# Linear attention and a highway layer on one core: each pair of output tiles stored by one transfer

## The chip, the cores and the metric

The kernel runs on one core of a Trainium2 chip. The metric is the device time of one execution in microseconds; lower is better. The kernel before takes 126.87 us, the median of three runs (126.06 to 127.11). A trace of one execution was taken by the hardware profiler; all durations below come from it.

The names of the engines in the profile are PE (TensorE, matrix products), PEld (its weight loads), DVE (VectorE), ACT (ScalarE), POOL (GpSimd) and SP (SyncE, which here only issues transfers). Transfers between DRAM and the on-chip memory SBUF run on the core's 16 DMA engines, whoever issues them. In this kernel SP and ACT issue them.

## The reference

Inputs are q, k and v of shape (8, 8, 576, 64), that is batch, heads, tokens, head width, in float32, and two weights of 512 x 512 with a bias of 512. First comes linear attention, for each batch and head:

```python
q_s = softmax(q, axis=-1)            # over the head width
k_s = softmax(k, axis=2)             # over the tokens
kv  = einsum('bhsd,bhse->bhde', k_s, v)
x   = einsum('bhsd,bhde->bhse', q_s, kv)
```

Then the heads are put side by side, which gives x of shape (4608, 512), and a highway layer follows:

```python
H = maximum(x @ w_h, 0)
T = sigmoid(x @ w_t + b_t)
out = T * H + (1 - T) * x            # (4608, 512), float32
```

## The kernel before

**Tokens and tiles.** A batch has 576 tokens, cut as 64 groups p of 9 tokens j: token 9p + j. A load of q, k or v puts two heads times the 64 groups on the 128 partitions, with four pairs of heads and nine tokens along each partition (`rows_of`, L182). The output is computed in 36 tiles of 128 tokens by 512 columns. For one batch there are four tiles jp = 0 to 3, each of 64 groups times two tokens (rows 0 to 63 hold one token of each group, rows 64 to 127 another). The ninth tokens of two batches make one tile together. So two batches are nine tiles, and four such rounds are 36.

**Steps.** Each batch passes these steps: `k`, `v`, `q` load it; `ek` and `eq` take exponentials on ACT; `vc` casts v to half precision on POOL, ACT or DVE; `kv` (L254) multiplies on TensorE; `kr` and `kn` divide by the sums; `qt` (L292) turns the exponentials of q with TensorE transposes, and `qc` (L301) copies them to SBUF on DVE or ACT. Each tile i then passes `xu` (L318, q times kv), `rs` and `x` (L333, division by the sums, giving x in half precision), `xt` (L340) and `xe` (L347), which turn x, `mt` (L367, times w_t) and `mh` (L375, times w_h), `th` (tanh of half the gate), `dd`, and then `uu` and `oo` (L426), which combine the parts into the output. Where a step `uu` has the suffix P, the product (L408) and one sum (`ee`, L401) run on POOL, otherwise a single DVE instruction (L410) takes their place. `fill` steps (L172) multiply zeros on TensorE, while data is still on the way.

**Stores.** Two neighbouring tiles share one output buffer of two times 512 columns (`mate`, L414; `oo` writes half of it). Tiles 31 to 34 are stored singly, and the last tile (35, ninth tokens) in two halves of its columns. Step `st` (L428) stores. For a pair it is called twice, with r = 0 and r = 1, and each call stores 64 partitions, with two tokens of each group that lie two apart. A single tile is also stored in two calls of 64 partitions. A tile of ninth tokens goes in one call of 128 partitions. The output buffers of pairs are seven (pool `op`, shared with the four landing buffers of the weights at the start); those of single tiles are three (L420).

**Order.** The list `ORDER` (L16) is the program: its steps are emitted one after the other, and every engine and every queue works through its own part of it in that order. A suffix A, D or P picks the engine. Nothing is reordered later. A store with suffix A is issued by ACT, all others and all loads by SP; an instruction that waits for its data holds back all that stand behind it on the same queue. Loads have three landing buffers for each of q, k and v.

Of the kernel before, what the change touches and what calls it, by code (L numbers as in the profile page):

```python
# [16 lines left out]
b_0 b_32 setuppool fill_30 fill_30 k_0_2 setupdve bsplit v_0_2 bp v_0_0 vc_0_0:D vc_0_1:D ek_0_2 k_0_0 vc_0_3:A ek_0_3
vc_0_2 kv_0_1 bc ek_0_0 kr_0_1 q_0_0 q_0_4 w_t_0 ek_0_1 kn_0_1 fill_30 w_h_2 kv_0_0 eq_0_0 bw_0 qt_0_0 kr_0_0 qc_0_0
kn_0_0 bw_1 eq_0_1 fill_16 w_h_0 xu_0_1 xu_0_0 xu_1_0 qt_0_1 w_t_2 fill_16 wtc_0 rs_0_1 rs_1_0 rs_0_0 q_1_0 x_1_0 whc_2
qc_0_1:A x_0_0 half v_1_0 xt_0_0 xe_0_0 x_0_1 xt_0_1 whd_3 whd_2 xe_0_1:D mt_0_0 xt_1_0 whc_0 k_1_0 wtc_2:D vc_1_1 k_1_2  # L20
xe_1_0 v_1_2 eq_0_2 whd_0 xu_3_0 eq_1_0 mh_0_1 vc_1_0 mt_0_1 q_1_4 mt_1_0 rs_3_0 q_2_0 x_3_0 th_0_0 ek_1_1 xu_2_0 whd_1
xt_3_0 ek_1_0 mh_0_0 rs_2_0 xe_3_0:D qt_1_0 bw_3 x_2_0 mh_1_0 dd_0 k_2_0 ee_0 xt_2_0 mh_3_0 vc_1_2 kv_1_0 v_2_0 dd_1
xe_2_0:D qc_1_0 th_1_0 ek_1_2 ek_1_3 mh_2_0 uu_0_0:P kr_1_0 mt_3_0 uu_1_0 vc_1_3:A bw_2 dd_3 qt_0_2 kn_1_0 th_3_0 oo_0_0
kv_1_1 mt_2_0 oo_1_0 bw_5 xu_4_0 uu_3_0:P kr_1_1 q_3_0 kn_1_1 qc_0_2 dd_2 xu_5_0 rs_5_0 eq_1_1 th_2_0 x_5_0 rs_4_0
qt_1_1 xt_5_0 x_4_0 xe_5_0:D qc_1_1:A bw_4 xu_6_0 ee_3 eq_1_2 xu_4_1 qt_1_2 rs_6_0 qc_1_2 eq_2_1 eq_2_2 xt_4_0 uu_2_0:P
xe_4_0 rs_4_1 k_3_0 x_6_0 x_4_1 mh_5_0 mt_5_0 xu_7_0 xt_4_1 dd_5 xe_4_1:D eq_2_0 mt_4_0 th_5_0 ek_2_2 qt_2_0 xt_6_0
rs_7_0 x_7_0 mt_4_1 ek_2_0 xu_8_0 xe_6_0:D uu_5_0 qc_2_0 xt_7_0 oo_3_0 mh_4_0 th_4_0 mh_6_0 rs_8_0 ee_2 oo_5_0 bw_6:A
xe_7_0:D vc_2_0:A x_8_0 mh_4_1 v_3_0 k_4_0 vc_2_2 mt_6_0 th_6_0 xt_8_0 kv_2_0 dd_6 dd_4 bw_7:A uu_6_0 kr_2_0 xe_8_0
kn_2_0 oo_2_0 mh_7_0 uu_4_0:P mt_7_0 dd_7 xu_9_0 ee_4 bw_8:A qt_2_1 rs_9_0 oo_4_0 eq_3_1 th_7_0 v_4_0 mt_8_0 x_9_0
xt_9_0 bw_9:A qc_2_1 eq_3_0 xu_10_0 ek_3_2 mh_8_0 q_4_0 xe_9_0:D rs_10_0 x_10_0 mt_9_0 dd_8 xu_11_0 qt_2_2 rs_11_0  # L30
xt_10_0 th_8_0 uu_7_0:P oo_6_0 x_11_0 ek_3_0 mh_9_0 vc_3_0 qc_2_2 uu_8_0 xe_10_0 xu_12_0 qt_3_0 xt_11_0 rs_12_0 vc_3_2:A
x_12_0 bw_10:A ee_7 dd_9 mh_10_0 xe_11_0:D v_5_0 th_9_0 kv_3_0 mt_10_0 bw_11:A qc_3_0 ek_4_2 st_1_0_0 ee_9 kr_3_0
xt_12_0 th_10_0 oo_7_0 oo_8_0 kn_3_0 qt_3_1 xe_12_0:D xu_13_0 k_5_0 eq_3_2 uu_9_0:P rs_13_0 x_13_0 st_3_0_1 oo_9_0
bw_12:A mh_11_0 mt_11_0 ek_4_0 th_11_0 dd_10 q_5_0 xu_14_0 vc_4_2 xt_13_0 xe_13_0 dd_11 rs_14_0 mt_12_0 uu_10_0:P
th_12_0 x_14_0 qc_3_1 mh_12_0 xu_15_0 vc_4_0:A eq_4_0 uu_11_0 rs_15_0 qt_3_2 x_15_0 mh_13_0 dd_12 xt_14_0 bw_13:A
xe_14_0:D kv_4_0 xt_15_0 eq_4_1 uu_12_0 qc_3_2 ee_10 st_1_0_1:A mh_14_0 kr_4_0 xe_15_0:D bw_14:A mt_13_0 kn_4_0 xu_16_0
th_13_0 oo_10_0 oo_11_0 eq_4_2 dd_13 v_6_0 rs_16_0 qt_4_0 x_16_0 qc_4_0:A uu_13_0 mt_14_0 oo_12_0 xt_16_0 xe_16_0
bw_16:A xu_17_0 dd_14 qt_4_1 mh_16_0 rs_17_0 k_6_0 x_17_0 vc_5_2 xu_18_0 qc_4_1 mh_15_0 th_14_0 rs_18_0 x_18_0 oo_13_0
bw_15:A mt_15_0 ee_14 ek_5_2 xu_20_0 ek_5_0 vc_5_0 xt_18_0 xe_18_0 dd_16 rs_20_0 x_20_0 mt_16_0 th_15_0 dd_15 xt_17_0
kv_5_0 th_16_0 xe_17_0:D mh_18_0 uu_14_0:P uu_16_0:P kr_5_0 q_6_0 eq_5_2 bw_18:A oo_14_0 uu_15_0 xt_20_0 kn_5_0 ee_16  # L40
qt_5_2 eq_5_1 mt_18_0 bw_17:A xe_20_0 qc_5_2 xu_19_0 dd_18 qt_4_2 th_18_0 rs_19_0 oo_15_0 x_19_0 qc_4_2:A uu_18_0
mh_17_0 mt_17_0 xt_19_0 eq_5_0 bw_20:A st_3_0_0 xu_21_0 q_7_0 dd_17 qt_5_0 th_17_0 xe_19_0:D qc_5_0:A rs_21_0 oo_16_0
mh_20_0 vc_6_0 uu_17_0 x_21_0 mt_20_0 bw_19:A ek_6_2 st_7_0_0 vc_6_2 dd_20 xt_21_0 xu_22_0 th_20_0 rs_22_0 bw_21:A
mt_19_0 st_5_0_0 xe_21_0 mh_19_0 oo_17_0 st_5_0_1 x_22_0 ek_6_0 xu_23_0 qt_5_1 rs_23_0 xt_22_0 eq_6_0 mh_21_0 x_23_0
xe_22_0:D kv_6_0 ee_20 dd_19 st_7_0_1 xt_23_0 v_7_0 uu_20_0:P dd_21 oo_18_0 qc_5_1 th_19_0 mt_21_0 th_21_0 ee_19 qt_6_0
bw_22:A k_7_0 st_14_0_1:A st_10_0_1 st_10_0_0 kr_6_0 kn_6_0 mh_22_0 uu_19_0:P uu_21_0 xu_24_0 xe_23_0:D rs_24_0 mt_22_0
st_8_0_0 eq_7_0 oo_19_0 th_22_0 x_24_0 qc_6_0 mh_23_0 bw_23:A oo_20_0 dd_22 xu_25_0 rs_25_0 qt_7_0 x_25_0 uu_22_0:P
eq_6_1 qc_7_0:A xt_24_0 mt_23_0 xe_24_0:D xu_26_0 dd_23 xt_25_0 th_23_0 st_12_0_0 oo_21_0 rs_26_0 x_26_0 qt_6_1 ee_22
xe_25_0 uu_23_0 mh_24_0 xt_26_0 vc_7_0 qc_6_1 xu_27_0 bw_24:A oo_22_0 rs_27_0 x_27_0 eq_7_1 mt_24_0 qt_7_1 xe_26_0
bw_25:A xu_29_0 th_24_0 bw_26:A rs_29_0 dd_24 ek_7_0 mt_25_0 st_21_0_0 x_29_0 mh_25_0 vc_7_2 dd_25 xt_27_0 ek_7_2  # L50
xu_28_0 mh_26_0 th_25_0 oo_23_0 rs_28_0 eq_7_2 st_14_0_0 mt_26_0 qc_7_1 st_21_0_1:A qt_7_2 x_28_0 xe_27_0 ee_24 th_26_0
uu_24_0:P kv_7_0 uu_25_0 bw_27:A mh_27_0 xt_28_0 dd_26 kr_7_0 kn_7_0 xe_28_0 eq_6_2 mt_27_0 oo_24_0 ee_26 xu_30_0
mh_28_0 st_12_0_1 uu_26_0:P dd_27 bw_28:A xt_29_0 mt_28_0 th_27_0 oo_25_0 qc_7_2:A rs_30_0 x_30_0 uu_27_0 st_23_0_1
xu_31_0 dd_28 xe_29_0 bw_29:A mh_29_0 xt_30_0 st_23_0_0:A rs_31_0 th_28_0 mt_29_0 x_31_0 xe_30_0 st_25_0_1 uu_28_0
xt_31_0 dd_29 xu_32_0 mh_30_0 th_29_0 st_19_0_1 bw_30:A rs_32_0 oo_26_0 x_32_0 st_16_0_1:A xe_31_0:D mt_30_0 st_19_0_0:A
xt_32_0 qt_6_2 th_30_0 oo_27_0 xu_33_0 st_17_0_0 dd_30 mh_31_0 oo_28_0 rs_33_0 bw_31:A xe_32_0 x_33_0 uu_29_0:P
st_26_0_0:A uu_30_0 mt_31_0 dd_31 xu_34_0 xt_33_0 ee_29 rs_34_0 qc_6_2:A bw_32:A st_28_0_1 xe_33_0:D mh_32_0 th_31_0
oo_29_0 st_16_0_0:A x_34_0 oo_30_0 mt_32_0 xu_35_0 uu_31_0 oo_31_0 xt_34_0 st_31_0_1 dd_32 th_32_0 uu_32_0 xe_34_0:D
st_28_0_0 mh_33_0 bw_33:A rs_35_0 mt_33_0 mh_34_0 bw_34:A x_35_0 dd_33 th_33_0 xt_35_0 uu_33_0 mt_34_0 st_31_0_0:A
xe_35_0:D oo_32_0 bw_35_1 dd_34 st_32_0_1 st_32_0_0 th_34_0 oo_33_0 mh_35_0 bw_35_0:A st_30_0_1 mt_35_1 st_25_0_0  # L60
uu_34_0 st_33_0_1:A th_35_1 st_30_0_0 dd_35 mt_35_0 th_35_0 st_33_0_0 uu_35_1 oo_34_0 oo_35_1 st_34_0_1 st_34_0_0:A
# [5 lines left out]
def kernel(  # L67
# [360 lines left out]
    def st(e, i, h, r):  # L428
        bs, jp = tiles[i]
        b = bs[r % len(bs)]  # L430
        cs, rows = columns(i, h), slice(NP * r, NP * r + NP)
        eng = nc.scalar if e == "A" else nc.sync
        dst = out[b * S:(b + 1) * S, cs].rearrange("(p j) n -> p j n", j=NJ)
        if mate(i) is not None:
            eng.dma_start(dst[:, 2 * jp + r - 2:2 * jp + r + 1:2], T[f"oo{i - 1}"][rows])
        elif len(bs) == 1:
            eng.dma_start(dst[:, 2 * jp + r], T[f"o{i}"][rows, cs])
        else:
            ends = out[b * S:(b + 2) * S, cs].rearrange("(r j) n -> r j n", j=NJ)
            eng.dma_start(ends[:, 8], T[f"o{i}"][:, cs])  # L440

# [40 lines left out]
```

## Time and profile before

| what | value |
|---|---|
| median of three runs | 126.87 us |
| the profiled execution's own time | 126.15 us |
| its span, first to last instruction | 124.40 us |
| TensorE busy | 113.7 us, 91% of the span |
| DVE, ACT, POOL busy | 97.4, 91.9, 87.7 us |
| read from DRAM, written | 30.41 MB, 9.44 MB |
| DMA packets | 20292 |

The page divides the span into 40 equal slices of 3.1 us; a digit is the busy share of an engine in tenths. Of the output's transfers, 28 carry pairs (256 KB each), eight carry single tiles (128 KB each), three carry ninth tokens (256 KB), and two the halves of the last tile (128 KB each). SP issues 29 of the 41 and ACT 12.

### The profile page before, as it was taken

Reading aid. Unit: us, or ns where it says so; the run is one execution under the profiler, and the core shown is the slowest. Engines: PE = TensorE matmul, PEld = TensorE weight load, DVE = VectorE, ACT = ScalarE, POOL = GpSimd, SP = SyncE. Lnnn points to the kernel's source line nnn. Section 1 sums busy time; section 2 is a strip of 40 time slices with the busy share of each in tenths; the row PEclk is TensorE's granted clock in tenths of the full one; section 3 lists DMA queues with packets and bytes.
Section 4 is the critical chain, followed back from the end, with each engine's and each line's share of the span. In section 5 each row is a group of like instructions: output and inputs, shape, how many; then the busy total and the mean of one; then the engine's idle time right before and its main releaser. Section 6 shows DMA issues by size and latency. Waiting matters only on the chain.

```text
span 124.4 us, 3617 instructions
## 1 busy us (share of the span) xinstructions
PE 113.7 (91%) x1447; PEld 71.3 (57%) x1447; DVE 97.4 (78%) x230; ACT 91.9 (74%) x144; POOL 87.7 (71%) x88
## 2 busy tenths in 40 slices
...
DMA  3999999999999999999999999999878309987993
GB/s 68 390 391 363 383 374 388 384 378 391 391 384 391 392 389 391 391 388 397 401 401 394 381 395 403 383 403 387 320 182 220 71 16 227 266 256 156 264 226 115
DMA packets 20292, 40.08 MB, mean 322 GB/s; under 512 B 1202, under 2 KB 3506, under 8 KB 20276
## 3 DMA queue, kind: packets, MB, share of 16 engines
...
q14 instruction: 5, 0.04, 0.1%
HBM read 30.41 MB, written 9.44 MB: 320 GB/s over the span
## 4 chain that ended last, share of the span: by engine, by line
PE 87%; DVE 5%; ACT 1%; issue 1%; POOL 0%; DVEq 0%; POOLq 0%
PE gps L375 24%; PE tps L367 24%; PE turned L172 12%; PE xu L318 7%; PE turned L340 7%; PE qps L292 6%; PE kv L254 5%; DVE u L410 1%; DVE d L395 1%; PE tps L357 1%; DVE x L333 1%; DVE o L426 1%; DVE w16t L206 0%; DVE w16h L212 0%; ACT tps L391 0%
## 5 line engine op out<-in xcount | busy, mean ns | idle before, releaser
L367 PE MATMUL tps<-w16t,xT 128*128 128x512 f16 (+1 forms) x148 | 37.1, 373 | 0.2 <-DVE w16t L206 0.2
L375 PE MATMUL gps<-w16h,xT 128*128 128x512 f16 x144 | 37.0, 379 | 0.0
L426 POOL TENSOR_TENSOR o<-u,x 128x512 f32<-128x512 f16 (+1 forms) x21 | 23.7, 1134 | 4.9 <-DVE u L410 4.9
L244 POOL CAST v<-v 128x1152 f16<-128x1152 f32 (+1 forms) x13 | 13.0, 1006 | 19.3 <-DMA v<-in_v_dram 19.3
L333 DVE TENSOR_TENSOR x<-xu,rs 128x512 f16<-128x512 f32 (+1 forms) x38 | 25.0, 660 | 1.9
L395 DVE SCALAR_TENSOR_TENSOR d<-x,gps 128x512 f16<-128x512 f16 x36 | 24.2, 678 | 0.8 <-PE gps L375 0.7
L367 PEld LDWEIGHTS <-xT 128*128 128x128 f16 x148 | 13.6, 98 | 12.5 <-issue 0.4
L238 ACT ACTIVATE ek<-k 128x1152 f16<-128x1152 f32 (+1 forms) x20 | 18.7, 963 | 2.4 <-DMA k<-in_k_dram 2.2
L401 POOL TENSOR_TENSOR e<-d,x 128x512 f16<-128x512 f16 x15 | 17.3, 1154 | 4.2 <-DVE d L395 4.2
L282 ACT ACTIVATE qe<-q 128x1024 f16<-128x1024 f32 (+1 forms) x24 | 19.9, 841 | 0.0
L375 PEld LDWEIGHTS <-xT 128*128 128x128 f16 x144 | 12.6, 98 | 10.3 <-DVE xT L347 0.3
L355 ACT COPY tps<-ball 128x512 f32<-128x512 f32 (+1 forms) x30 | 17.6, 585 | 0.5 <-DVE u L410 0.3
L408 POOL TENSOR_TENSOR u<-th,d 128x512 f16<-128x512 f16 x15 | 17.4, 1157 | 0.5 <-POOL u L408 0.4
L426 POOL TENSOR_TENSOR o<-u,e 128x512 f32<-128x512 f16 x15 | 17.3, 1153 | 0.6
L391 ACT ACTIVATE tps<-tps 128x512 f32<-128x512 f32 (+1 forms) x22 | 12.4, 562 | 7.1 <-PE tps L367 6.8
L172 PE MATMUL turned<-blank 128*128 128x256 f16 x122 | 15.9, 295 | 1.3 <-POOL blank L151 1.3
L410 DVE SCALAR_TENSOR_TENSOR u<-tps,d 128x512 f16<-128x512 f32 (+1 forms) x22 | 14.4, 660 | 1.4 <-ACT tps L391 0.6
L340 PE MATMUL turned<-idh,x 128*128 128x128 f16 x144 | 14.3, 219 | 1.3 <-DVE x L333 0.8
L172 PEld LDWEIGHTS <-blank 128*128 128x128 f16 x122 | 12.7, 106 | 3.7 <-POOL blank L151 1.3
L318 PE MATMUL xu<-kvb,eq 128*128 128x130 f16 (+1 forms) x160 | 14.2, 224 | 0.1
L340 PEld LDWEIGHTS <-x 128*128 128x128 f16 x144 | 10.1, 98 | 6.9 <-DVE x L333 2.2
L318 PEld LDWEIGHTS <-eq 128*128 128x128 f16 (+1 forms) x160 | 10.0, 101 | 6.7 <-DVE x L333 1.8
...
## 6 DMA issues: line engine op xcount, KB each, us to landing
...
out_dram<-o SPq DMA_DIRECT2D x23, 256.0 KB, 10.1
...
out_dram<-o ACTq DMA_DIRECT2D x8, 256.0 KB, 5.5
...
```

Of the source, the lines that this page charges most:

```text
L172: nc.tensor.matmul(spare, blank[:, 0:P], blank[:, 0:2 * P], start=True, stop=True, skip_group_check=True)
L238: nc.scalar.activation(t[:, :, c:c + n].rearrange("p j c d -> p c j d"), T[f"k32{b}"][:, c:c + n].rearrange("p c (j d) -> p c j d", j=NJ), ...
L282: nc.scalar.activation(t[:, j0:j1].rearrange("p j c d -> p c j d"), T[f"q32{b}"].rearrange("p c (j d) -> p c j d", j=NJ)[:, :, j0:j1], AF.Exp)
L318: nc.tensor.matmul(dst, T[f"eq{b}_{jp // 2}"][:, jp % 2, n], kvb[b % NKV][:, hh, kk], start=True, stop=True, skip_group_check=True)
L333: nc.vector.tensor_mul(t[:, k0:k1], sums(i, k)[:, :, :, 0:64], T[f"rs{i}_{k}"][:, 0:k1 - k0].unsqueeze(3).to_broadcast([P, k1 - k0, 4, D]))
L340: nc.tensor.matmul(t[:, n], T[f"x{i}"][:, n * P:(n + 1) * P], idh, is_transpose=True, start=True, stop=True, skip_group_check=True)
L355: nc.scalar.copy(t[:, cs], ball[:, cs])
L367: nc.tensor.matmul(T[gate(i, k)][:, cs], T[f"xT{i}"][:, n], w16["t"][:, n, cs], start=False, stop=(n == parts[-1] and not first), skip_gro ...
L375: nc.tensor.matmul(t, T[f"xT{i}"][:, n], w16["h"][:, n], start=(first and n == parts[0]), stop=(n == parts[-1] and not (first and len(part ...
L395: nc.vector.scalar_tensor_tensor(t, T[f"x{i}"], -0.5, T[f"gps{i}"], op0=ALU.mult, op1=ALU.max)
L408: eng.tensor_mul(t, T[f"th{i}"], T[f"d{i}"])
L426: eng.tensor_add(t[:, cs], T[f"u{i}"][:, cs], T[f"{'e' if lifted(i) else 'x'}{i}"][:, cs])
```

## The change

The two tokens of each group that share a tile are no longer neighbours: tile jp now holds tokens j and j + 2, so that the two tiles of a pair together give, in each partition of their common buffer, two tokens that lie side by side in DRAM, 4096 bytes. Step `st` loses its argument r. A pair is stored by one transfer of 128 partitions with 4096 bytes each (512 KB), a single tile by one transfer of 128 partitions with 2048 bytes each (256 KB). The tiles of ninth tokens are stored as before. That leaves 23 store steps, 19 on SP and 4 on ACT.

The list of steps is a new one. Its loads begin with q, v and k of batch 0 (before: k, v, k, q). It has 99 multiplications of zeros in its `fill` steps (before 122), 17 tiles with their product on POOL (before 15), and 12 copies of `qc` on ACT (before 8). The stores among the loads stand as follows, with the other steps left out:

```
... q_5_0 st_1_0 v_6_0 k_6_0 q_6_0 st_3_0:A q_7_0 st_5_0 k_7_0 st_7_0 st_10_0 v_7_0
st_19_0 st_21_0:A st_12_0 st_16_0 st_14_0 st_23_0 st_26_0 st_17_0 st_8_0:A st_25_0
st_28_0 st_31_0 st_33_0 st_30_0 st_32_0 st_34_0 st_35_0 st_35_1:A
```

A second way of turning q, by DMA transposes (`dt`), is defined as well, for batches named by steps `dt_` in the list. The list has no such step, so `BY_DMA` is empty.

```diff
     def qt(e, b, g):
...
                 nc.tensor.matmul(
-                    t[:, (j - j0) // 2, 2 * kk:2 * kk + 2, (j - j0) % 2],
+                    t[:, (j - j0) % 2, 2 * kk:2 * kk + 2, (j - j0) // 2],
                     T[f"qe{b}"][:, j, 2 * kk:2 * kk + 2].rearrange("p c d -> p (c d)"), idh,
...
+    def turned_q(b, jp, n):
+        if b not in BY_DMA:
+            return T[f"eq{b}_{jp // 2}"][:, jp % 2, n]
...
     def xu(e, i, k):
...
-                nc.tensor.matmul(dst, T[f"eq{b}_{jp // 2}"][:, jp % 2, n], kvb[b % NKV][:, hh, kk],
+                nc.tensor.matmul(dst, turned_q(b, jp, n), kvb[b % NKV][:, hh, kk],
...
-    def st(e, i, h, r):
+    def st(e, i, h):
         bs, jp = tiles[i]
-        b = bs[r % len(bs)]
-        cs, rows = columns(i, h), slice(NP * r, NP * r + NP)
+        b, cs = bs[0], columns(i, h)
         eng = nc.scalar if e == "A" else nc.sync
-        dst = out[b * S:(b + 1) * S, cs].rearrange("(p j) n -> p j n", j=NJ)
-        if mate(i) is not None:
-            eng.dma_start(dst[:, 2 * jp + r - 2:2 * jp + r + 1:2], T[f"oo{i - 1}"][rows])
-        elif len(bs) == 1:
-            eng.dma_start(dst[:, 2 * jp + r], T[f"o{i}"][rows, cs])
-        else:
+        if len(bs) == 2:
             ends = out[b * S:(b + 2) * S, cs].rearrange("(r j) n -> r j n", j=NJ)
             eng.dma_start(ends[:, 8], T[f"o{i}"][:, cs])
+            return
+        if mate(i) is None:
+            rows = out[b * S:(b + 1) * S].rearrange("(p j) n -> j p n", j=NJ)
+            a, step = (2 * jp, 1) if b in BY_DMA else (4 * (jp // 2) + jp % 2, 2)
+            eng.dma_start(rows[a:a + step + 1:step], T[f"o{i}"])
+        else:
+            rows = out[b * S:(b + 1) * S].rearrange("(p j) n -> p (j n)", j=NJ)
+            a = 4 * (jp // 2) * DM
+            eng.dma_start(rows[:, a:a + 4 * DM].rearrange("p (r n) -> r p n", r=2),
+                          T[f"oo{i - 1}"].rearrange("p a n -> p (a n)"))
```

More of the change, by code (lines that the diff above doesn't have):

```diff
@@ L16 @@
 ORDER = """
[L17 to L61, printed above, removed]
@@ L62 @@
-uu_35_0 oo_35_0:D st_35_0_0 st_35_1_0:A
+b_0 b_32 q_0_0 setuppool v_0_0 k_0_0 setupdve half eq_0_0 bsplit fill_16 k_0_2 fill_12 qt_0_0 bp ek_0_1 ek_0_0 fill_12
+fill_16 vc_0_1:A qc_0_0 fill_6 vc_0_0 ek_0_3 v_0_2 kv_0_0 vc_0_2:A kr_0_0 vc_0_3:D kn_0_0 fill_12 ek_0_2 q_0_4 kv_0_1
+eq_0_1 kr_0_1 kn_0_1 xu_0_0 w_t_0 fill_9 bc qt_0_1 xu_0_1 rs_0_1 xu_1_0 bw_0 w_h_2 rs_1_0 rs_0_0 w_t_2 q_1_0 eq_0_2
+fill_16 wtc_2:P wtc_0:D qc_0_1:A x_1_0 xt_1_0 x_0_0 whc_2 xu_3_0 bw_1 x_0_1 xe_1_0 w_h_0 xt_0_0 xt_0_1 v_1_0 xe_0_1
@@ new lines @@
+rs_3_0 xe_0_0 mt_1_0 mt_0_0 mt_0_1 k_1_0 x_3_0 xt_3_0 eq_1_0 whc_0 qt_1_0 th_0_0 vc_1_0 whd_0 bw_3 whd_1 k_1_2 whd_2
+whd_3 xu_2_0 xe_3_0 mh_0_0 mh_0_1 qc_1_0:A vc_1_1:D ek_1_1 v_1_2 mh_1_0 dd_0 rs_2_0 qt_0_2 ek_1_0 q_1_4 ee_0 x_2_0
+th_1_0 qc_0_2:A mt_3_0 ek_1_2 ek_1_3 dd_1 uu_0_0:P vc_1_3:A q_2_0 k_2_0 xt_2_0 vc_1_2 th_3_0 xe_2_0:D uu_1_0 mh_3_0 dd_3
+uu_3_0:P kv_1_0 bw_2 eq_1_1 mh_2_0 eq_1_2 kr_1_0 kv_1_1 kn_1_0 kr_1_1 v_2_0 mt_2_0 xu_4_0 bw_4 kn_1_1 xu_5_0 dd_2 qt_1_1
+rs_5_0 th_2_0 qc_1_1:A oo_0_0 ee_2 oo_1_0 rs_4_0 x_5_0 xu_4_1 ee_3 bw_5 uu_2_0:P x_4_0 rs_4_1 xt_5_0 q_3_0 xe_5_0:D
@@ new lines @@
+k_3_0 xu_6_0 mh_5_0 rs_6_0 x_4_1 xt_4_0 oo_3_0 xt_4_1 eq_2_0 mt_5_0 x_6_0 xe_4_0:D dd_5 mt_4_0 xu_7_0 xe_4_1:D mt_4_1
+rs_7_0 eq_2_1 th_5_0 xt_6_0 x_7_0 mh_4_1 mh_4_0 qt_1_2 eq_2_2 xe_6_0:D uu_5_0 qc_1_2 xt_7_0 ek_2_2 ek_2_0 oo_2_0 mh_6_0
+xu_8_0 dd_4 oo_5_0 rs_8_0 th_4_0 xe_7_0:D qt_2_0 bw_6:A x_8_0 mt_6_0 vc_2_0:A vc_2_2 bw_7:A v_3_0 th_6_0 uu_4_0:P bw_8:A
+qc_2_0 xt_8_0 kv_2_0 k_4_0 dd_6 mh_7_0 kr_2_0 kn_2_0 v_4_0 xe_8_0:D mt_7_0 dd_7 ee_6 eq_3_2 eq_3_1 uu_6_0:P xu_9_0 ee_4
+q_4_0 qt_2_1 v_5_0 rs_9_0 x_9_0 oo_4_0 mt_8_0 th_7_0 ee_7 xu_10_0 qc_2_1 oo_6_0 rs_10_0 xt_9_0 eq_3_0 x_10_0 mh_8_0
@@ new lines @@
+bw_9:A dd_8 xe_9_0 qt_2_2 xu_12_0 rs_12_0 x_12_0 mt_9_0 mh_9_0 xt_10_0 qc_2_2 vc_3_0 xe_10_0:D xu_11_0 uu_7_0:P ek_3_2
+rs_11_0 qt_3_0 th_8_0 ek_3_0 x_11_0 oo_7_0 uu_8_0 k_5_0 vc_3_2:A q_5_0 mh_10_0 dd_9 kv_3_0 kr_3_0 oo_8_0 xt_11_0 kn_3_0
+qc_3_0:A bw_10:A ee_9 st_1_0 xe_11_0:D qt_3_1 mt_10_0 th_9_0 qc_3_1:A dd_10 xu_13_0 bw_11:A xt_12_0 mh_11_0 v_6_0
+th_10_0 ek_4_0 mt_11_0 rs_13_0 x_13_0 xu_14_0 k_6_0 xe_12_0:D xt_13_0 uu_10_0 uu_9_0:P rs_14_0 mh_12_0 xe_13_0:D x_14_0
+bw_12:A dd_12 mt_12_0 th_11_0 dd_11 xu_15_0 bw_13:A vc_4_2 xt_14_0 th_12_0 oo_9_0 ek_4_2 eq_4_0 mt_13_0 mh_13_0 rs_15_0
@@ new lines @@
+x_15_0 xe_14_0:D xu_16_0 uu_12_0 oo_10_0 qt_3_2 q_6_0 rs_16_0 mh_14_0 bw_14:A xt_15_0 mt_14_0 dd_13 th_13_0 eq_4_2
+vc_4_0 x_16_0 dd_14 uu_13_0 uu_11_0:P st_3_0:A qc_3_2:A xe_15_0:D oo_12_0 eq_4_1 kv_4_0 qt_4_0 mh_15_0 kr_4_0 xt_16_0
+kn_4_0 oo_13_0 th_14_0 qc_4_0:A ee_11 xu_17_0 bw_15:A uu_14_0 xe_16_0:D rs_17_0 ek_5_2 qt_4_1 mt_15_0 vc_5_0 oo_11_0
+x_17_0 dd_15 ee_15 xu_18_0 bw_16:A vc_5_2 mh_16_0 th_15_0 qc_4_1 ek_5_0 rs_18_0 x_18_0 xt_17_0 xe_17_0:D mt_16_0
+uu_15_0:P xu_20_0 oo_15_0 q_7_0 eq_5_2 xt_18_0 rs_20_0 x_20_0 eq_5_0 qt_5_2 bw_17:A mh_17_0 xe_18_0 kv_5_0 th_16_0
@@ new lines @@
+xt_20_0 dd_16 dd_17 qc_5_2:A xe_20_0 mt_17_0 qt_4_2 kr_5_0 uu_16_0 kn_5_0 mh_20_0 qc_4_2 oo_14_0 bw_18:A xu_21_0 th_17_0
+bw_21:A eq_5_1 rs_21_0 st_5_0 qt_5_0 ee_17 qc_5_0:A mt_18_0 th_18_0 x_21_0 bw_20:A vc_6_2 dd_20 oo_16_0 xu_19_0 mh_18_0
+rs_19_0 xt_21_0 qt_5_1 uu_17_0:P x_19_0 qc_5_1 xu_22_0 xe_21_0 mt_20_0 rs_22_0 k_7_0 ek_6_0 oo_17_0 x_22_0 th_20_0
+st_7_0 mh_21_0 ek_6_2 xt_22_0 st_10_0 dd_18 xu_23_0 xe_22_0:D vc_6_0 rs_23_0 x_23_0 dd_21 mt_21_0 mh_22_0 ee_18 uu_20_0
+uu_18_0:P th_21_0 xt_23_0 bw_22:A xe_23_0:D dd_22 kv_6_0 eq_6_0 mt_22_0 xt_19_0 eq_6_1 kr_6_0 kn_6_0 xe_19_0:D mh_23_0
@@ new lines @@
+bw_23:A dd_23 oo_18_0 ee_21 qt_6_0 xu_24_0 mh_19_0 uu_21_0:P qc_6_0 rs_24_0 th_22_0 eq_7_1 mt_23_0 eq_7_0 x_24_0 bw_19:A
+oo_20_0 oo_21_0 th_23_0 xu_25_0 dd_19 xt_24_0 qt_7_0 rs_25_0 mt_19_0 xe_24_0:D x_25_0 xt_25_0 uu_23_0 xu_26_0 qc_7_0:A
+th_19_0 qt_6_1 ee_22 mh_24_0 rs_26_0 v_7_0 xe_25_0 x_26_0 xu_27_0 uu_22_0:P uu_19_0 dd_24 mh_25_0 ek_7_2 eq_6_2 xt_26_0
+bw_25:A oo_19_0 oo_23_0 xe_26_0 rs_27_0 qc_6_1 mt_25_0 x_27_0 bw_24:A th_25_0 mh_26_0 dd_25 xu_29_0 xt_27_0 mt_24_0
+bw_26:A rs_29_0 oo_22_0 qt_7_1 x_29_0 xu_28_0 dd_26 xe_27_0:D mt_26_0 rs_28_0 xt_29_0 st_19_0 vc_7_2 ek_7_0 th_24_0
@@ new lines @@
+vc_7_0:A uu_25_0:P st_21_0:A ee_25 uu_24_0 x_28_0 xe_29_0 mh_27_0 dd_27 st_12_0 st_16_0 kv_7_0 mh_29_0 oo_25_0 bw_27:A
+th_26_0 kr_7_0 st_14_0 uu_26_0 oo_24_0 kn_7_0 xt_28_0 mt_27_0 xe_28_0 xu_30_0 bw_28:A rs_30_0 dd_29 qc_7_1:A oo_26_0
+mh_28_0 st_23_0 x_30_0 mt_28_0 th_27_0 dd_28 xu_31_0 rs_31_0 bw_29:A xt_30_0 x_31_0 ee_27 eq_7_2 qt_6_2 th_28_0 xe_30_0
+mt_29_0 uu_27_0:P bw_30:A th_29_0 xu_32_0 xt_31_0 oo_27_0 qc_6_2 rs_32_0 qt_7_2 mh_30_0 st_26_0 st_17_0 x_32_0 uu_29_0
+xu_33_0 rs_33_0 xe_31_0:D ee_28 st_8_0:A mt_30_0 qc_7_2 mh_31_0 x_33_0 bw_31:A th_30_0 xu_34_0 oo_29_0 rs_34_0 dd_30
@@ new lines @@
+xt_33_0 x_34_0 uu_28_0:P bw_33:A mt_31_0 dd_31 xe_33_0 xt_32_0 th_31_0 uu_31_0 ee_30 xe_32_0 mh_33_0 xu_35_0 oo_28_0
+st_25_0 bw_32:A mt_33_0 rs_35_0 th_33_0 dd_33 uu_30_0:P xt_34_0 oo_31_0 mt_32_0 mh_32_0 xe_34_0 x_35_0 th_32_0 uu_33_0
+mh_34_0 bw_34:A xt_35_0 st_28_0 dd_32 oo_33_0 xe_35_0 uu_32_0 bw_35_0:A mt_34_0 th_34_0 mh_35_0 mt_35_0 oo_30_0 st_31_0
+st_33_0 dd_34 st_30_0 oo_32_0 uu_34_0 dd_35 oo_34_0 bw_35_1 th_35_0 st_32_0 mt_35_1 st_34_0 th_35_1 uu_35_0 uu_35_1
+oo_35_0:D st_35_0 oo_35_1:D st_35_1:A
```

19 lines of the change are left out of this document (17 added, 2 removed).

## The prediction

> **What bounds the kernel now.** I read the page first: shares by engine, slices, chain.
>
> ```profile
> PE 113.7 (91%) x1447; PEld 71.3 (57%) x1447; DVE 97.4 (78%) x230; ACT 91.9 (74%) x144; POOL 87.7 (71%) x88
> ...
> DMA  3999999999999999999999999999878309987993
> GB/s 68 390 391 363 383 374 388 384 378 391 391 384 391 392 389 391 391 388 397 401 401 394 381 395 403 383 403 387 320 182 220 71 16 227 266 256 156 264 226 115
> ...
> HBM read 30.41 MB, written 9.44 MB: 320 GB/s over the span
> ...
> PE 87%; DVE 5%; ACT 1%; issue 1%; POOL 0%; DVEq 0%; POOLq 0%
> ```
>
> TensorE holds 87% of the chain that ended last, so the time is matmul time. But the DMA row is full for 28 slices of 3.1 us, some 87 us. TensorE bounds the kernel with the DMA engines close behind, and the kernel bears a DMA loss only while the transfers stay on all 16 engines. Next the windows: the loads' stage (mostly loads) and a late stage that has stores alone. Columns: stretch, its length, busy time of PE, PEld, DVE, ACT and POOL with counts, granted clock, DMA share, GB/s.
>
> ```profile
> 40.00:60.00 20.00, 20.00 (x360) 12.19 (x357) 18.50 (x40) 19.49 (x29) 18.45 (x18) 1.00 1.05 392
> 103.00:110.00 7.00, 7.00 (x53) 3.88 (x51) 6.20 (x14) 4.36 (x9) 6.48 (x6) 1.00 0.99 262
> ```
>
> Full DMA engines move 392 GB/s of loads, which is 392/16 = 24.5 GB/s per engine, but only 262 GB/s of stores. The trace's record of single packets says why: a 2048-byte store packet takes 84 ns alone (24.4 GB/s) and about 160 ns (median 156, 75th percentile 166) in 103 to 117 us. [...]
>
> Last the issues and the end of SP's queue:
>
> ```profile
> out_dram<-o SPq DMA_DIRECT2D x23, 256.0 KB, 10.1
> out_dram<-o ACTq DMA_DIRECT2D x8, 256.0 KB, 5.5
> ...
> 117.07 2.54 SPq L437 DMA_DIRECT2D out_dram<-o  x2
> 119.70 1.09 SPq L440 DMA_DIRECT2D out_dram<-o  x1
> ```
>
> The last addition (L426) ends at 118.2 by the timeline. Its SP store is issued at 119.70, because two stores ahead take 2.54 us. The span ends at 124.4.
>
> [...]
>
> **The change part by part.** *The pair stores (L435, st).* Before, each of 14 pairs leaves in two transfers: DRAM side 64 x 2 x 512, SBUF side 64 partitions. After, the DRAM side is arranged as "r p n" with r = 2 outermost: 2 rows of step 1024 elements, then 64 of step 4608, then 1024 elements. These can't merge into 128 (2 x 1024 isn't 4608). The SBUF side begins with 128. [...] So 512 KB go through engines 0 and 1 alone, 64 packets of 4096 bytes each. The four single tiles (31 to 34) become "j p n" with 2 outermost: [...] 64 packets of 2048 bytes on each. The ninth tokens and the last tile keep 128 outermost, so 16 engines.
>
> *Price of a packet.* Undisturbed medians in the packet records: 1024 bytes 46 ns, 1280 55, 2048 84, 2304 93. A line through the first and last is 8.4 ns + 0.0367 ns per byte, which gives 84 for 2048, as recorded, and 159 for 4096 (estimate; 25.8 GB/s). Bounds: 168 ns, twice the 2048-byte packet[...]. I take 159: the four sizes lie on the line[...].
>
> *Sum on engine 0 (engine 1 is the same).* Pairs: 14 x 64 x 159 ns = 142.5 us. Singles: 4 x 64 x 84 ns = 21.5 us. Ninth tokens and last tile, an eighth of 64 packets each: 3 x 8 x 84 ns + 2 x 8 x 46 ns = 2.8 us. Its share of loads: 30.41 MB / 16 = 1.90 MB at 24.5 GB/s = 77.6 us. Together 244.4 us of work on one engine. Today its part of the stores lies among 16, and it has room.
>
> *What lies beside it.* All of the compute, about 114 us to the last matmul. The engine must stay fed for this sum to be the time. The stores of the new list stand between loads: st_1 before v_6; st_3 (on ACT) and st_5 between q_6 and k_7; st_7 and st_10 before v_7. Up to q_5 the engine has its share of loads, 62 us. Then st_1 10.2, v_6, k_6 and q_6 9, st_3 10.2, q_7 3, st_5 10.2, k_7 3, st_7 and st_10 20.4, v_7 3: v_7 lands at about 131 us. The loads are whole only when engines 0 and 1 have done their share, so 14 idle engines don't help. What remains is nine pairs (92 us), four singles (21.5) and the rest (2.8): 131 + 116 = 247. The output buffers (seven pairs, three single tiles) hold the compute back: tile 27's addition waits for st_12 (about 162 us), tile 29's for st_14 (about 182). From 182 us on st_23, st_25, st_28 and the small ones keep the engine fed while the last six tiles pass, at some 2.6 us each (93 us of matmuls over 36 tiles). So I find no gap, and put 0 to 20 us as its bound.
>
> *Sum against the profiled execution (126.15 us; span 124.40, so 1.75 around it; the median of the runs, 126.87, is 0.72 above it).* Start: the first 5 us moved 191 GB/s, which loses 2.6 us against 392. End: SP's last issue ends at 120.8 and the span at 124.4; 3 us without the transfer itself (estimate). 244.4 + 2.6 + 3 = 250.0 span, +1.75 = 251.8: I say 252 for the median too, since 0.7 is less than the error of a packet's price.
>
> *The other edits.* The turned tiles (L293) put tokens j and j+2 instead of j and j+1 in a tile: as many transposes, copies (L302) and multiplications (L318) of the same size, so 0. The paths for DMA transposes run nowhere, since the list has no such step: 0. The list: fills fall from 122 to 99; four copies of q (L301, 0.56 on DVE, 0.78 on ACT) go from DVE to ACT, 3.1 us more there; two more tiles have their product and sum on POOL (L401 and L408, 4.6 us more); eight fewer store issues of about 0.6 us on ACT's queue. With the pair stores as the bound the engines idle for half the time, which covers all of it; without that cover the second rival prices it.
>
> **The rivals.** (a) *One engine is slower than I think*: an engine that stores alone may manage only 262/16 = 16.4 GB/s. Then 4.19 MB cost 256 us, and with 77.6 + 2.8 + 5.6 + 1.75 the time is 343. Against it: the 84 ns packets. Chance 0.04. (b) *All 16 engines carry the new stores*, on the other side of today's time. The place is the store's split: if it takes the 128 partitions instead of the outer 2, [...] the stores go at about 392 instead of 262 GB/s. [...] Then TensorE stays the bound: 23 fewer fills of 0.113 us (30 in 3.38 us on the chain) are 2.6 us, and the last store no longer stands 1.5 us (118.2 to 119.7) behind two half-tile stores: 126.15 - 4.1 = 122.0. For it: every transfer that this trace shows ran wide, and none shows another count. [...] The forecast itself is the case in which the change doesn't do what it says. Chance 0.10. (c) *Two engines each time, but different ones*: transfers then overlap, and only the last ones show. Tile 30's sum comes at about 116, plus 10.2 and 3 us: 129 us. [...] chance 0.04.
>
> **How the numbers follow.** Forecast 0.82, (a) 0.04, (b) 0.10, (c) 0.04. Range: [...] High end: 168 ns packets add 8 us, gaps 20, so 280. That holds 0.80 of the 0.82; (a), (b) and (c) are left out. Under 1% is what a measurement here can't tell from no change. Faster by over 1%: 0.08 of (b). Within: 0.01 of (b) and 0.01 of (c). Slower: 0.90.
>
> **What would show it.** The GB/s row falls to about 50 and the DMA digit to 1 over the second half (2 of 16 engines); the mean over the span is 160 GB/s. The 512 KB stores take at least 10 us to land, their median over 20. The last load of v lands near 131 us. GpSimd's addition waits for stores, and TensorE's busy share falls below 50%. If the 512 KB stores land in 3 to 5 us, the engine count was wrong; if they land in 10 us but beside each other, (c); if the DMA row has empty slices after 60 us, the gaps were mis-sized.

## The result, and the profile after

The changed kernel takes 246.19 us, the median of four runs (245.91 to 246.33), against 126.47 us for the kernel before in the same comparison. The ratio is 1.946, with a 95% interval of 1.935 to 1.956. The forecast was 252 us with a range of 234 to 280; the low end was an estimate of the author's, and no view of before shows it. The ratios in this text leave out single executions that ran in a slower state, so they are not always the quotient of the medians printed beside them.

The profiled execution took 246.33 us, with a span of 244.6 us. Its page answers to the lines shown of before: busy shares, DMA slices (now 6.1 us each), traffic, and the chain that ended last by engine and by line.

```profile
PE 123.1 (50%) x1424; PEld 73.1 (30%) x1424; DVE 94.8 (39%) x225; ACT 95.8 (39%) x148; POOL 91.9 (38%) x91
...
DMA  6999999999861926112511111121131111111110
GB/s 229 383 377 391 381 389 392 388 390 391 331 215 65 331 108 222 55 52 69 205 52 56 52 53 53 52 93 53 52 128 53 52 52 53 52 51 71 53 71 37
...
HBM read 30.41 MB, written 9.44 MB: 163 GB/s over the span
...
DMA 57%; PE 19%; POOL 8%; DVE 4%; SPq 2%; issue 1%; ACT 1%; DVEq 0%; POOLq 0%
DMA out_dram<-o 57%; POOL o L445 5%; PE gps L392 5%; PE turned L170 4%; PE tps L384 4%; PE qps L298 1%; POOL u L425 1%; PE turned L357 1%; PE kv L252 1%; PE xu L335 1%; SPq L458 1%; SPq L462 1%; DVE x L350 1%; DVE kvb L270 1%; POOL e L418 1%
```

The traffic is the same as before, and the second to the tenth slice are as before: about 390 GB/s with full DMA engines. Then the stores begin, and from the seventeenth slice the row rests at 52 to 53 GB/s with a digit of 1, with short peaks where loads or small stores run beside. That is one eighth of the engines (2 of 16) and about one eighth of the rate. The chain has turned over: TensorE held 87% of it, and now the stores hold 57%.

Three more views show how the stores hold the rest back. The first is a stretch of the windows (length, busy times of PE, PEld, DVE, ACT, POOL, clock, DMA share, GB/s). The second is the list of waits (waiting engine and line, what for, us in total, times, longest). The third is two lines of the timeline, one of GpSimd and one of SP's queue.

```profile
195.00:205.00 10.00, 1.43 (x7) 0.68 (x5) 2.02 (x4) 0.74 (x2) 1.49 (x2) 0.50 0.13 52
```

```profile
POOL o L445 <- DMA out_dram<-o: 93.3, 7, 25.5
...
PE tps L384 <- ACT tps L372: 39.3, 2, 21.8
...
ACT tps L372 <- DVE u L427: 23.0, 3, 22.5
```

```profile
131.12 1.14 POOL L242 CAST v<-v 128x1152 f16<-128x1152 f32 x1 [10.68 <-DMA v<-in_v_dram]
...
114.59 53.64 SPq L462 DMA_DIRECT2D out_dram<-o  x5
```

The share of 0.13 in the window is 2/16. GpSimd waits 93.3 us for output buffers that are still being stored, and DVE, ACT and TensorE wait in turn behind it. The last v landed at 131.1 us. SP needed 53.64 us to issue five stores, 3.7 to 26.6 us for one.

Two more counts show the engines themselves. The first is the page's count of packets under 512 bytes, here for before, for after, and for the old kernel with the new form of store, which comes below:

```profile
DMA packets 20292, 40.08 MB, mean 322 GB/s; under 512 B 1202, under 2 KB 3506, under 8 KB 20276
DMA packets 17960, 40.07 MB, mean 164 GB/s; under 512 B 662, under 2 KB 2966, under 8 KB 17944
DMA packets 19900, 40.07 MB, mean 174 GB/s; under 512 B 810, under 2 KB 3114, under 8 KB 19884
```

Suppose that a store leaves one such small packet for each engine that it runs on. Before, 41 stores on 16 engines give 41 x 16 = 656. After, 5 stores on 16 and 18 on two give 5 x 16 + 18 x 2 = 116. The difference is 540, and the page has 1202 - 662 = 540. In the third kernel 28 stores have two instead of 16, which is 28 x 14 = 392 fewer, and the page has 1202 - 810 = 392. The kernels of all other experiments fit to within one packet.

The second is the trace's records of single packets, with start and length. In after, two or more data packets are in flight from 2 us to 242.8 us, but for gaps below 0.1 us, and where no load and no small store runs it is two, with overlaps of a few ns. A pair alone on the way takes 10.3 us. From 134.9 to 154.5 us a pair of SP's queue and one of ACT's are on the way together, still with two packets in flight, and the one of ACT takes 19.6 us. So stores of both queues use the same two engines. A store that is spread over 16 engines waits for them as well: of the 128 packets of the ninth tokens issued by ACT, 112 start within 1.0 us (161.7 to 162.6), and the last 16, two sixteenths, between 164.3 and 166.1, behind the pairs.

### The profile page after: what moved, and what is told of

The parts are those of the page before. It is cut to its first block, busy times and chain, and to the rows that moved or that the text cites. A ratio compares the mean times of both kernels' runs of the same rounds, so it can differ in the third digit from the quotient of the medians.

```text
span 244.6 us, 3538 instructions
## 1 busy us (share of the span) xinstructions
PE 123.1 (50%) x1424; PEld 73.1 (30%) x1424; DVE 94.8 (39%) x225; ACT 95.8 (39%) x148; POOL 91.9 (38%) x91
## 3 DMA queue, kind: packets, MB, share of 16 engines
HBM read 30.41 MB, written 9.44 MB: 163 GB/s over the span
## 4 chain that ended last, share of the span: by engine, by line
DMA 57%; PE 19%; POOL 8%; DVE 4%; SPq 2%; issue 1%; ACT 1%; DVEq 0%; POOLq 0%
DMA out_dram<-o 57%; POOL o L445 5%; PE gps L392 5%; PE turned L170 4%; PE tps L384 4%; PE qps L298 1%; POOL u L425 1%; PE turned L357 1%; PE kv L252 1%; PE xu L335 1%; SPq L458 1%; SPq L462 1%; DVE x L350 1%; DVE kvb L270 1%; POOL e L418 1%
## 5 line engine op out<-in xcount | busy, mean ns | idle before, releaser
L384 PE MATMUL tps<-w16t,xT 128*128 128x512 f16 (+1 forms) x148 | 41.4, 408 | 39.4 <-ACT tps L372 39.3
L445 POOL TENSOR_TENSOR o<-u,x 128x512 f32<-128x512 f16 x18 | 20.7, 1155 | 72.9 <-DMA out_dram<-o 72.6
L392 PE MATMUL gps<-w16h,xT 128*128 128x512 f16 x144 | 40.5, 410 | 0.1
L384 PEld LDWEIGHTS <-xT 128*128 128x128 f16 x148 | 14.3, 106 | 52.2 <-issue 43.1
L445 POOL TENSOR_TENSOR o<-u,e 128x512 f32<-128x512 f16 x17 | 19.6, 1155 | 21.1 <-DMA out_dram<-o 20.7
L335 PE MATMUL xu<-kvb,eq 128*128 128x130 f16 (+1 forms) x160 | 15.6, 236 | 16.0 <-DVE x L350 15.8
L418 POOL TENSOR_TENSOR e<-d,x 128x512 f16<-128x512 f16 x17 | 19.7, 1157 | 2.9 <-DVE d L412 2.9
L425 POOL TENSOR_TENSOR u<-th,d 128x512 f16<-128x512 f16 x17 | 19.7, 1159 | 0.4 <-ACT th L406 0.4
L392 PEld LDWEIGHTS <-xT 128*128 128x128 f16 x144 | 13.7, 104 | 13.8 <-issue 3.3
L170 PE MATMUL turned<-blank 128*128 128x256 f16 x99 | 14.2, 310 | 1.3 <-POOL blank L149 1.3
L252 PE MATMUL kv<-v,ek 64*64 64x65 f16 x576 | 7.0, 199 | 15.2 <-ACT v L242 15.0
```

What stands on the lines that cost most here:

```text
L170: nc.tensor.matmul(spare, blank[:, 0:P], blank[:, 0:2 * P], start=True, stop=True, skip_group_check=True)
L335: nc.tensor.matmul(dst, turned_q(b, jp, n), kvb[b % NKV][:, hh, kk], start=True, stop=True, skip_group_check=True)
L384: nc.tensor.matmul(T[gate(i, k)][:, cs], T[f"xT{i}"][:, n], w16["t"][:, n, cs], start=False, stop=(n == parts[-1] and not first), skip_gro ...
L392: nc.tensor.matmul(t, T[f"xT{i}"][:, n], w16["h"][:, n], start=(first and n == parts[0]), stop=(n == parts[-1] and not (first and len(part ...
L418: eng.tensor_add(T[f"e{i}"], T[f"d{i}"], T[f"x{i}"])
L425: eng.tensor_mul(t, T[f"th{i}"], T[f"d{i}"])
```

## The experiments

Three theories were tried against each other. T1 is the forecast's: a transfer whose DRAM side begins with a count of 2 runs on two DMA engines. T2 says that the new list and its waits are the cause. T3 says that packets of 4096 bytes, or stores of 512 KB, are slow by themselves.

**The same list, layout and packets, with 64 outermost.** Each store is cut in its two halves of 64 partitions:

```diff
-            eng.dma_start(rows[a:a + step + 1:step], T[f"o{i}"])
+            for r in range(2):
+                eng.dma_start(rows[a + step * r], T[f"o{i}"][NP * r:NP * r + NP])
...
-            eng.dma_start(rows[:, a:a + 4 * DM].rearrange("p (r n) -> r p n", r=2),
-                          T[f"oo{i - 1}"].rearrange("p a n -> p (a n)"))
+            both = T[f"oo{i - 1}"].rearrange("p a n -> p (a n)")
+            for r in range(2):
+                eng.dma_start(rows[:, a + 2 * DM * r:a + 2 * DM * (r + 1)], both[NP * r:NP * r + NP])
```

> The changed kernel with its list and its layout of tokens, but each pair and each single tile stored by two transfers of 64 partitions (still 4096 bytes per partition for a pair), one behind the other on the same queue. Theory (T1: engines 0 and 1 carry the outer-2 transfers alone): the DRAM side now begins with 64, so all 16 engines share each store, and TensorE bounds the kernel again: 123 us, between 120 and 128. Rival T2 (the new list with its waits on SP's queue is the cause): stays near 246. Rival T3 (a packet of 4096 bytes or a store of 512 KB is slow by itself): near 240.

Measured: 123.72 us (123.57 to 123.98, four runs) against 125.80; ratio 0.981, interval 0.970 to 0.991. The page of this kernel has the rate of before again, and no stage at 52 GB/s:

```profile
PE 112.4 (92%) x1424; PEld 69.2 (57%) x1424; DVE 93.4 (77%) x225; ACT 95.7 (79%) x148; POOL 92.1 (76%) x91
...
GB/s 63 363 395 377 386 365 391 396 369 389 390 389 390 392 389 389 395 386 391 393 404 399 395 392 387 402 399 407 315 24 248 304 255 237 337 95 194 211 232 141
```

With list and packet size unchanged the 122 us of slowdown are gone, as T1 had it. This excludes T2 and the packet part of T3.

**The old list, layout and packets, with 2 outermost.** The two store steps of a pair each take one tile of 128 partitions; nothing else of the kernel before is touched:

```diff
-            eng.dma_start(dst[:, 2 * jp + r - 2:2 * jp + r + 1:2], T[f"oo{i - 1}"][rows])
+            j = 2 * jp - 2 + 2 * r
+            eng.dma_start(dst[:, j:j + 2].rearrange("p s n -> s p n"), T[f"oo{i - 1}"][:, r])
```

> The kernel before with its list, its layout and its 2048-byte packets; only the two store steps of a pair now store one tile each, 128 partitions, with the DRAM side 2 x 64 x 512 (outermost 2). T1: 28 transfers of 64 packets of 84 ns on each of engines 0 and 1 are 150.5 us, the other stores 5.5, the loads 75 to 79; with 7 us around it 238 us, between 228 and 248. T2 and T3: 127, since neither list nor packet size has changed.

Measured: 232.39 us in one run, inside the range expected. The form of the transfer alone makes the kernel before nearly as slow as after, with 256 KB stores of 2048-byte packets. A quiet stretch of its windows has the signature of after:

```profile
170.00:174.00 4.00, 0.00 (x0) 0.00 (x0) 0.00 (x0) 0.00 (x0) 0.00 (x0) 0.50 0.13 51
```

**Half of the pairs.** The first experiment's kernel, but seven pairs keep the changed kernel's transfer:

```diff
+            if i in (1, 5, 10, 14, 19, 23, 28):
+                eng.dma_start(rows[:, a:a + 4 * DM].rearrange("p (r n) -> r p n", r=2), both)
+                return
             for r in range(2):
```

> The changed kernel with seven of its fourteen pairs (those stored by st_1, 5, 10, 14, 19, 23, 28) left on the outer-2 transfer and everything else in halves of 64 partitions. T1: the sum on engine 0 is 7 x 64 x 157 ns = 70 us, the other pairs 9 to 18, the rest 5.5, loads 75 to 79, and 7 around it: 170 us, between 164 and 178. T2: 246. T3: near 240, since the packets are all of 4096 bytes.

Measured: 170.25 us in one run. The sum on one engine, now with 70 us of pairs, gives the time, while the list with its waits is that of after. That the point is met so closely is partly luck, since the other pairs alone stood in the sum with 9 to 18 us.

**The four single tiles alone.** All pairs in halves, tiles 31 to 34 as the changed kernel stores them:

```diff
-            eng.dma_start(rows[:, a:a + 4 * DM].rearrange("p (r n) -> r p n", r=2),
-                          T[f"oo{i - 1}"].rearrange("p a n -> p (a n)"))
+            both = T[f"oo{i - 1}"].rearrange("p a n -> p (a n)")
+            for r in range(2):
+                eng.dma_start(rows[:, a + 2 * DM * r:a + 2 * DM * (r + 1)], both[NP * r:NP * r + NP])
```

> The changed kernel with all pairs in halves of 64 partitions, and only the four single tiles (31 to 34) on the outer-2 transfer. T1: nothing is late before the end; there four stores of 5.4 us stand behind each other on engines 0 and 1, from about 111 us when tile 31 is summed: 111 + 21.5 + 5 = 137 us, between 130 and 142. T2: 246. T3: about 123 to 127, as these packets have 2048 bytes.

Measured: 140.22 us in one run, 3 us over the point. Four of 23 stores cost some 16 us, because at the end nothing else is left to run beside them. The windows of the end show two engines at work and all others idle:

```profile
128.00:134.00 6.00, 0.00 (x0) 0.00 (x0) 0.00 (x0) 0.00 (x0) 0.00 (x0) 0.50 0.13 51
```

The packet records show where the 3 us went. The packets of the four tiles start at 112.1 us instead of 111, and the two engines also carry their part of the pair and of the last tile stored at the same time, so they are done at 137.0 us; put were 111 + 21.5 = 132.5. The end after that is shorter than put.

**Where the 2% of the halves come from.** The first experiment is faster than before. Two kernels split its list from its packets. One has the new list with the old layout and the old 2048-byte halves:

```diff
-                    t[:, (j - j0) % 2, 2 * kk:2 * kk + 2, (j - j0) // 2],
+                    t[:, (j - j0) // 2, 2 * kk:2 * kk + 2, (j - j0) % 2],
...
+        dst = out[b * S:(b + 1) * S].rearrange("(p j) n -> p j n", j=NJ)
+        for r in range(2):
+            half = slice(NP * r, NP * r + NP)
+            if mate(i) is None:
+                eng.dma_start(dst[:, 2 * jp + r], T[f"o{i}"][half])
+            else:
+                eng.dma_start(dst[:, 2 * jp + r - 2:2 * jp + r + 1:2], T[f"oo{i - 1}"][half])
```

> The new list of steps with the old layout of tokens and the old stores (two transfers of 64 partitions with twice 2048 bytes, one behind the other at each store step). It asks what the list alone is worth. T1 with the list as the gain of the first experiment (123.7 against 125.8): 123.7, within 0.7 of it. Rival: the gain came from packets of 4096 bytes: 125.8, as before.

The other has the old list and the new layout:

```diff
-                    t[:, (j - j0) // 2, 2 * kk:2 * kk + 2, (j - j0) % 2],
+                    t[:, (j - j0) % 2, 2 * kk:2 * kk + 2, (j - j0) // 2],
...
-            eng.dma_start(dst[:, 2 * jp + r - 2:2 * jp + r + 1:2], T[f"oo{i - 1}"][rows])
+            eng.dma_start(dst[:, 4 * (jp // 2) + 2 * r:4 * (jp // 2) + 2 * r + 2], T[f"oo{i - 1}"][rows])
...
-            eng.dma_start(dst[:, 2 * jp + r], T[f"o{i}"][rows, cs])
+            eng.dma_start(dst[:, 4 * (jp // 2) + jp % 2 + 2 * r], T[f"o{i}"][rows, cs])
```

> The counterpart: the old list with its split stores, but the new layout, so that a half pair leaves in packets of 4096 bytes. If the list made the gain of the first experiment: 125.8, within 0.7. If the packets made it: 123.7.

Measured: 123.80 us with the list alone (ratio 0.980, interval 0.974 to 0.987), and 126.07 us with the packets alone (ratio 1.0008, interval 0.9975 to 1.0041). The list makes the gain, and larger packets from 64 partitions are worth nothing that can be measured. By the timelines, one profile each, the last matmul ends at 115.1 us with the new list and at 116.5 in the kernel before, and from the last addition to the end of the span 5.1 us pass instead of 6.2.

**One transfer of 128 partitions that does use 16 engines.** The copies of the turned q put a tile's rows in the order 2p + r, and the DRAM side becomes 64 x 2 x 1024:

```diff
-        copy(t.rearrange("p a n t -> p (a n t)"), T[f"qps{b}_{g}"].rearrange("p a n s t -> p (a n s t)"))
+        copy(t.rearrange("p a n (t s) -> p (a n) s t", s=s), T[f"qps{b}_{g}"].rearrange("p a n s t -> p (a n) s t"))
...
-            eng.dma_start(rows[a:a + step + 1:step], T[f"o{i}"])
+            eng.dma_start(rows[a:a + step + 1:step].rearrange("r p n -> p r n"), T[f"o{i}"])
...
-            eng.dma_start(rows[:, a:a + 4 * DM].rearrange("p (r n) -> r p n", r=2),
+            eng.dma_start(rows[:, a:a + 4 * DM].rearrange("p (r n) -> p r n", r=2),
```

> The changed kernel with one transfer per pair as intended, but with 64 as the outermost count on the DRAM side: the copies of the turned q put the rows of a tile in the order 2p + r instead of 64r + p, so that the transfer can be written as 64 x 2 x 1024. T1: 16 engines and both halves of the partitions at once, stores near 390 GB/s instead of 262, so the end is 1 to 2 us shorter than in the first experiment: 122 us, between 119.5 and 124; a copy of q on VectorE with scattered writes may cost 1.1 us instead of 0.6, which other work covers. T2 and T3 (list, or size of packet or transfer): 240 to 246, since list, packet and transfer size are those of the changed kernel.

Measured: 124.45 us (124.32 to 125.25, four runs); ratio 0.988, interval 0.982 to 0.994. That is above the range expected, 119.5 to 124, but it excludes what was left of T3: stores of 512 KB in 4096-byte packets, from the same list, are not slow. The stretch from 93 to 100 us, which by the packet records holds stores of pairs alone, is shown first for this kernel and then for the halves:

```profile
93.00:100.00 7.00, 7.00 (x123) 4.23 (x121) 5.94 (x14) 5.75 (x9) 6.92 (x7) 1.00 1.01 399
```

```profile
93.00:100.00 7.00, 7.00 (x120) 4.16 (x119) 5.76 (x14) 5.87 (x10) 6.92 (x7) 1.00 0.86 286
```

The faster stores bring no gain over the halves, though: the last matmul ends at 117.2 us instead of 115.1, and from the last addition to the end 3.7 us pass instead of 4.9. The copies, whose cost the expectation took as covered (its 1.1 us for one on VectorE was a guess), have become longer. Line L307, the copies of q, in this kernel and in the halves (ns of one: min, median, max):

```profile
L307 DVE COPY eq<-qps x12: 280/1283/1318, 6.7 to 106.4; 128x1024 f16<-128x1024 f16 x7, 128x256 f16<-128x256 f16 x5
L307 ACT COPY eq<-qps x12: 363/1316/1332, 15.0 to 100.6; 128x1024 f16<-128x1024 f16 x9, 128x256 f16<-128x256 f16 x3
```

```profile
L307 DVE COPY eq<-qps x12: 281/660/692, 7.8 to 104.3; 128x1024 f16<-128x1024 f16 x7, 128x256 f16<-128x256 f16 x5
L307 ACT COPY eq<-qps x12: 363/1012/1032, 16.0 to 98.7; 128x1024 f16<-128x1024 f16 x9, 128x256 f16<-128x256 f16 x3
```

With scattered writes a large copy takes 1.28 instead of 0.66 us on DVE and 1.32 instead of 1.01 on ACT. That these copies make the matmuls late is likely and not shown, since no kernel has them together with stores in halves.

**Whole transfers only at the end.** The cheap part of the last two kernels was put together: order 2p + r and whole transfers for the batches from `first` on, halves for those ahead; `first` stands for the number written there in each kernel. The single tiles, all of the last batch, are stored whole in both.

```diff
+        if b >= first:
+            copy(t.rearrange("p a n (t s) -> p (a n) s t", s=s), T[f"qps{b}_{g}"].rearrange("p a n s t -> p (a n) s t"))
+        else:
+            copy(t.rearrange("p a n t -> p (a n t)"), T[f"qps{b}_{g}"].rearrange("p a n s t -> p (a n s t)"))
...
+            if b >= first:
+                eng.dma_start(rows[:, a:a + 4 * DM].rearrange("p (r n) -> p r n", r=2), both)
+                return
```

With `first` = 6, the last two batches:

> Rows 2p + r and whole transfers (64 outermost on the DRAM side) for the last two batches alone, halves of 64 partitions for the first six. The kernel with rows 2p + r everywhere ended 1.2 us sooner after its last addition than the one in halves (3.7 against 4.9 us), but its matmuls ended 2 us later, which I put down to copies of 1.3 us in place of about 0.7 to 1.0. If that is so, a quarter of the slow copies costs 0.5 us and the shorter end stays: 123.0 us, about 0.7 below the halves. Rival: the later matmuls have nothing to do with the copies (their order on the engines or the stores' landing): no gain, 124.4.

With `first` = 7, the last batch:

> The same for the last batch alone (its four single tiles, 31 to 34, are the last stores but two). If the copies were the cost, the matmuls end as in halves, and the end is shorter by up to 1.2 us: 122.7. Rival as before: 123.7 to 124.4.

And the halves on the same chip:

> The kernel in halves of 64 partitions once more, on the same chip as the two others, so that less than a microsecond can be compared: 123.7.

Measured, six runs each, against 126.16 us before:

| kernel | us | range | ratio to before, 95% interval | last matmul ends | from the last sum to the end |
|---|---|---|---|---|---|
| halves everywhere | 124.00 | 123.66 to 124.35 | 0.984, 0.979 to 0.989 | 115.2 | 5.1 |
| last batch whole | 123.32 | 122.95 to 124.27 | 0.980, 0.974 to 0.985 | 115.8 | 4.2 |
| last two whole | 123.20 | 122.36 to 123.61 | 0.977, 0.971 to 0.984 | 116.2 | 3.1 |

The two right columns are from one profile each; the kernel with all batches whole has 117.2 and 3.7 there. In these profiles the matmuls end the later the more copies are scattered, and whole stores shorten the end. The sizes were missed: the matmuls were to end 0.5 us later with two batches and not at all with one, and came 1.0 and 0.6 us later, and the last batch alone was to be the faster of the two. The last two batches give the fastest kernel of this study, 0.8 us below the halves; the ranges don't meet, but the intervals of the ratios overlap, so its lead over the halves is likely and not settled.

## Why the prediction was right

**The engine count held.** It was the one step that no view of before could show: an assumption of the author's for a count of 2 that stands outermost. Window shares of 0.13 and 52 GB/s after, the count of small packets, two packets in flight, the cure by halves, the illness put into the old kernel, and the dose of seven pairs all say two engines. Stores issued by ACT do not escape: the pairs of SP and ACT from 134.9 to 154.5 us share two packets in flight. That excludes rival (c), whose transfers would overlap. Which two of the sixteen engines they are, no run shows; the numbers 0 and 1 of the forecast and of T1 were assumed as well.

**The packet held, its pace a little less.** The packet records of after have all 1792 packets of 4096 bytes at a median of 159 ns, the value read off the line through the smaller ones. But two engines move 52.4 GB/s (195 to 205 us), which is 26.2 per engine and 156 ns from one packet to the next: packets overlap by 3 ns. The pairs cost 140 us instead of 142.5, the singles about 20 instead of 21.5 (1.05 MB at 52 GB/s).

**What was off: the pace, and what lies around the sum.** With 140 + 20 + 2.8 for the stores and 30.41 MB at 390 GB/s (78.0) for the loads, the engine's work is 240.8 us instead of 244.4. That is the larger part of the miss, 3.6 us. The span of 244.6 leaves 3.8 us for start and end, where 5.6 were put. The first slice alone loses 2.5 us (229 against 390 GB/s for 6.1 us), so the estimated 3 us at the end were really about 1.3; the records agree, for the last packet ends at 243.2 us. The two parts are 5.4 of the 6 us between 252 and 246; the rest is rounding.

**One reading of before was wrong.** The packet records count from 10.7 us before the first instruction. The stretch "103 to 117 us", with a median of 156 ns, thus lies at 92 to 106 us of the span. In 103 to 110 us of the span, the stretch of 262 GB/s, a 2048-byte packet takes 84 ns in the median and 162 at the 75th percentile; the mean is 123. So some of the packets take longer in that stretch, and the mean grows by half, not to twice its size; what lengthens them, no view shows. That fits the rates (392/262 is 1.5). The price of a 4096-byte packet came from undisturbed ones and does not change.

**No gap: held.** The DMA row has no empty slice between the first store and the last slice, and the packet records have two packets in flight throughout. The last v landed at 131.1 us for a forecast of about 131. When the output buffers come free was put too late: GpSimd's addition for tile 27 ran at 146.75 us instead of 162, the one for tile 29 at 160.9 instead of 182. The stores were not early: the last packets of the second and fourth of the five that follow the last load on SP's queue end at 160.1 and 180.6 us, within 2 us of what was put for st_12 and st_14. The additions ran as soon as the first and the second were through (145.6 and 160.1). Why these freed them was not traced. It made no difference, since the queue was fed in any case. TensorE was forecast below half of the span and has 50%, a near miss. The landing times that were to show the 10 us are missing from the page for these stores; the packet records have 10.3 us for a pair alone and 19.6 for one beside another.

**The other edits.** They were put at nothing under cover, and no view contradicts that: with two-engine stores TensorE idles for half the span. Without the cover, the second rival had put the list at 4.1 us, 2.6 from the fills and 1.5 at the end. Measured without the two-engine stores it is 2.1 to 2.2 us in the medians and, between the profiles, 1.4 at the last matmul and about 1.1 at the end. So 23 fewer fills did not bring the matmuls forward by the 2.6 us put for them; how much of the 1.4 us is theirs and how much is the rest of the list, no run separates. The rival's first part, stores at about 392 GB/s, an estimate from the rate of the loads, was met at 399 by the kernel with whole transfers on 16 engines.

## What to carry to other kernels

Before a store is merged into "one transfer of 128 partitions", read the access pattern of its DRAM side as the instruction carries it. Here a count of 2 that stood outermost in DRAM left two DMA engines at work (share 0.13, 52 GB/s) although the store read all 128 partitions. With 64 outermost all 16 worked (share 1.01, 399 GB/s). Write the pattern so that the large count stands first, or keep the two halves as two transfers; here that is the difference between 246 and 124 us. Add up the bytes per DMA engine as one adds up instructions per compute engine. In the profile, look for a DMA share that rests far below 1 while stores are waiting (0.13 here, 2 of 16), and compare the counts of small packets.

## What the runs showed beyond that

Packets of 4096 bytes instead of 2048, from 64 partitions over 16 engines, changed nothing that can be measured (ratio 1.0008, 0.9975 to 1.0041). Whole transfers from 128 partitions did change the stores' rate: 286 GB/s at a share of 0.86 from halves, 399 GB/s at 1.01 from whole ones. Scaled to a full share that is about 333 against 395 GB/s, and a packet takes 196 against 166 ns in the mean. Why is not shown: whole transfers cover all 128 partitions, but they are also fewer and larger.

The granted clock of TensorE fell to 0.50 in the idle stretches of the slow kernels (the windows above), and the mean matmul of L384 took 408 ns instead of the 373 in the kernel with halves. TensorE was waiting for most of that time, so this costs little here, but the busy time of a stalled engine is not its work: 123.1 us after against 112.4 for the same list with halves.
